# Layer norm scalars moved to GpSimd without a reciprocal, the mean taken from the product's accumulator, the softmax sums' addition in the accumulating form, and new priorities

## The chip, the cores and the metric

One core of one Trainium2 chip runs the kernel. Its engines are PE (TensorE, matrix products), DVE (VectorE), ACT (ScalarE), POOL (GpSimd) and SP (SyncE, which here only issues DMAs). Each engine works through its own instructions in order, and waits on semaphores where another engine or a DMA must come first. The metric is the device time of one execution in microseconds (us), the median of several.

## The reference

Block-causal attention over 8 batches, 8 heads, 576 positions of 64 values, in blocks of 64, then one dense layer pair on 4608 tokens of 512 values, with a SoLU activation and a layer norm between:

```python
scores = scale * np.matmul(q, k.transpose(0, 1, 3, 2))
scores = np.where(block_i >= block_j, scores, -1000000000.0)
scores = scores - np.max(scores, axis=-1, keepdims=True)
attn = np.exp(scores)
attn = attn / (np.sum(attn, axis=-1, keepdims=True) + 1e-09)
x = np.matmul(attn, v)              # then (tokens, 512)
h = x @ w_in                        # (4608, 1024)
e = np.exp(h - np.max(h, axis=-1, keepdims=True))
solu = h * e / (np.sum(e, axis=-1, keepdims=True) + 1e-09)
mu = np.mean(solu, axis=-1, keepdims=True)
var = np.mean((solu - mu) ** 2, axis=-1, keepdims=True)
out = ((solu - mu) / np.sqrt(var + 1e-06) * g_ln) @ w_out
```

## The kernel before

**Attention.** Two heads make a pair; there are 32 pairs, and the first four are done in two parts. For a pair, q and k come by DMA into `qz` and `kz`, which hold two pairs at a time and exist once, so that they are loaded anew every second pair. DVE transposes them there (L535), and ACT, POOL and DVE split each into a high and a low part (`qh`, `ql`, `kh`, `kl`, L536 to L542; the diagonal copies `qdh` and `qdl` for the last 64 rows, L546). PE multiplies three products per score tile (L576; the last 64 rows of both heads in L570) into PSUM. DVE takes each row's maximum (`nm`, L605), ACT the exponential with its sum (`pb`, `z`, L617). DVE adds 1e-9 and inverts the sums (L627, L628), and the rows are scaled on POOL, DVE or ACT (L635 to L637). Except for the first eight pairs, DVE transposes `pb` in blocks (L643) and SP moves it to `pt` (L651). PE multiplies `pt` by `vr` (v, loaded by SP, L475 and L479): the attention product, L663, 52 instructions a pair. Its result is copied from PSUM to `xt` (L417 on ACT or L418 on DVE).

**The two dense layers ("MoE" in the names).** 36 tiles of 128 tokens. `xh` and `xl` are the high and low part of x (L726, L730). PE multiplies by `w_in` in two halves of 12 matmuls (L751, bank `ps` of two). DVE takes the maximum (L757), ACT the exponential with its sum in `m1` (L758), DVE the product h * e with its sum (L759, `m2`). L760 turns the sum into minus the mean, and L766 or L767 adds it to the tile `ub`. ACT squares with a sum (L769, `m4`). L772 to L774 work out 1/z and 1/(z * z * 1024), L777 the variance, and POOL the power -0.5 and the product with 1/z (L780, L781); that number scales the output (L825 or L826). For tiles 4 to 34 DVE transposes `ub` to `zb` (L787) and SP moves it to `ct` (L791); then come its high and low part, `ch` and `cl` (L799 to L803), and the product with `w_out` in two halves of 12 matmuls (L821). The other tiles are transposed on PE (L809).

**PSUM.** Two double banks (1024 columns; `ps_61`, `ps_62` in the order) take the tiles of L751 and L570; four single banks (`ps_63` to `ps_66`) take scores, attention products, output products and PE transposes, each as it comes free.

**The order** is not written by hand. A list scheduler in the kernel (`Schedule.run`) goes through a time of its own. Whenever an engine is free it takes, among the operations whose inputs are there, the one with the smallest key: a pair's or tile's number plus a constant of `PARAMS` for that kind of operation. Operations with alternatives may go to another engine (the constants that begin with `a_`, added to the key). `port=True` marks DVE operations that the scheduler does not let run beside POOL. All engines then execute the recorded order, whatever the real times are. The weights are split into parts in the same way at the start (`prep`, L355 to L385).

## Time and profile before

| what | value |
|---|---|
| median of the runs | 718.22 us (717.61 to 718.95, 3 runs) |
| the profiled execution | 716.22 us, its span 714.3 us |
| mean granted PE clock | 0.970 |
| instructions | 14282 |

A line of a group reads: line, engine, operation, written and read tensor, shape, count | busy us in all, mean ns of one | idle time of the engine just before them, and what ended it. A line of the timeline reads: start us, length us, engine, line, operation, and in brackets the idle time before it and its releaser. SPq is SP issuing a DMA. Line numbers are those of the kernel before.

### The profile page before, as it was taken

The page shows a single profiled execution, that of the slowest core. Times are in us where ns is not written, and L with a number is a line of the kernel's source. Part 1 is how long each engine was busy: PE and PEld are TensorE (multiplying, and loading weights), DVE is VectorE, ACT ScalarE, POOL GpSimd, SP SyncE. Part 2 cuts the span into 40 slices and gives each one's busy share as a digit, 9 for nine tenths or more (in the row PEclk, how much of TensorE's full clock was granted, in tenths as well). Part 3 has the DMA queues.
Part 4 walks back from the last instruction along what each step waited for, and adds up shares of the span by engine and source line. Part 5 has one row for each costly group of instructions (what it writes and reads, how often), then busy time and mean ns, then how long its engine had stood idle before and what let it go on. Part 6 is the DMA issues. An engine that isn't in the chain of part 4 may idle for free.

```text
span 714.3 us, 14282 instructions
## 1 busy us (share of the span) xinstructions
PE 673.9 (94%) x4747; PEld 530.8 (74%) x4747; DVE 593.2 (83%) x1353; ACT 453.7 (64%) x1136; POOL 353.3 (49%) x497
## 2 busy tenths in 40 slices
PE   5879979999989999999999998999999899999997
PEld 5657767877767877777777776777777677888886
DVE  2888999998989999898989997979898898555652
ACT  3888898876686657566666665666656566333332
POOL 2257567552555475555656565454646553133210
PEclk8698979999999999999999999999999999999999
...
GB/s 181 191 94 131 115 127 110 143 187 160 157 186 170 178 191 195 174 178 176 192 179 191 163 194 173 179 157 180 179 170 183 167 175 160 122 71 86 63 74 45
DMA packets 223434, 109.74 MB, mean 154 GB/s; under 512 B 186496, under 2 KB 202368, under 8 KB 223360
## 3 DMA queue, kind: packets, MB, share of 16 engines
...
## 4 chain that ended last, share of the span: by engine, by line
PE 29%; DVE 23%; DMA 6%; ACT 5%; issue 5%; SPq 4%; POOL 1%; DVEq 0%; POOLq 0%; ACTq 0%
PE ps L821 12%; PE ps L751 11%; DVE pb L643 6%; DMA qz<-in_q_dram 5%; DVE nm L605 5%; SPq L464 4%; PE ps L663 3%; DVE ms L757 2%; DVE ub L759 2%; PE ps L576 2%; ACT pb L637 2%; ACT pb L617 2%; DVE zb L787 1%; DVE qz L535 1%; ACT ub L758 1%
## 5 line engine op out<-in xcount | busy, mean ns | idle before, releaser
L617 ACT ACTIVATE pb<-ps,nm 128x256 f32<-128x256 f32 (+4 forms) x288 | 157.2, 554 | 103.0 <-DVE nm L605 69.7
L605 DVE TENSOR_REDUCE nm<-ps 128x1 f32<-128x256 f32 (+4 forms) x288 | 132.6, 507 | 0.2
L643 DVE STREAM_TRANSPOSE pb<-pb 128x1536 f32<-128x1536 f32 (+1 forms) x56 | 101.5, 1827 | 2.3 <-ACT pb L637 2.1
L663 PEld LDWEIGHTS ps<-pt,vr 128*64 128x64 f32 x1648 | 82.5, 140 | 19.0 <-issue 4.6
L663 PE MATMUL ps<-pt,vr 128*64 128x128 f32 (+1 forms) x1648 | 94.8, 273 | 0.1
L821 PE MATMUL ps<-woh,ch 128*128 128x512 f32 x288 | 81.7, 405 | 9.8 <-ACT pb L617 8.6
L751 PE MATMUL ps<-wih,xh 128*128 128x512 f32 x288 | 82.8, 409 | 4.6 <-DVE ub L759 2.6
L637 ACT ACTIVATE pb<-pb,rz 128x128 f32<-128x128 f32 (+4 forms) x166 | 84.8, 573 | 2.9 <-DVE rz L628 2.8
L803 POOL TENSOR_TENSOR cl<-ct,ch 128x512 fp32r<-128x512 f32 x52 | 66.6, 1289 | 33.9 <-ACT ch L799 30.0
L821 PE MATMUL ps<-wol,ch 128*128 128x512 f32 x288 | 79.5, 398 | 0.0
L821 PE MATMUL ps<-woh,cl 128*128 128x512 f32 x288 | 79.0, 396 | 0.0
L751 PE MATMUL ps<-wil,xh 128*128 128x512 f32 x288 | 78.8, 395 | 0.0
L751 PE MATMUL ps<-wih,xl 128*128 128x512 f32 x288 | 78.6, 394 | 0.0
L821 PEld LDWEIGHTS ps<-woh,ch 128*128 128x128 f32 x288 | 51.4, 189 | 25.2 <-POOL qdh L546 9.0
L751 PEld LDWEIGHTS ps<-wih,xh 128*128 128x128 f32 x288 | 50.9, 188 | 24.7 <-issue 8.4
L576 PE MATMUL ps<-kh,qh 64*128 64x128 f32 (+3 forms) x256 | 57.5, 385 | 9.5 <-ACT pb L617 7.9
L821 PEld LDWEIGHTS ps<-wol,ch 128*128 128x128 f32 x288 | 54.8, 190 | 12.9
L821 PEld LDWEIGHTS ps<-woh,cl 128*128 128x128 f32 x288 | 54.7, 190 | 12.9
L751 PEld LDWEIGHTS ps<-wih,xl 128*128 128x128 f32 x288 | 54.1, 188 | 12.9
L751 PEld LDWEIGHTS ps<-wil,xh 128*128 128x128 f32 x288 | 54.2, 188 | 12.8
L769 ACT ACTIVATE junk<-ub 128x1024 bf16<-128x1024 f32 x31 | 32.8, 1057 | 42.6 <-DVE ub L767 21.0
L758 ACT ACTIVATE ub<-ps,ms 128x1024 f32<-128x1024 f32 x36 | 40.0, 1111 | 29.2 <-DVE ms L757 29.2
...
## 6 DMA issues: line engine op xcount, KB each, us to landing
pt<-pb SPq DMA_DIRECT2D x112, 400.0 KB, 6.1
...
```

Source lines behind the costliest of these rows:

```text
L464: SP.dma_start(dst[32 * g : 32 * g + 32].rearrange("p m (g d) -> p (m g) d", d=32), src[b0, ha + g - g % 2 : ha + g - g % 2 + 2, :, 32 * ( ...
L576: PE.matmul(PS(sps[h])[:, off : off + 128 * (i_ + 1)], w_[half[h], 128 * i_ : 128 * i_ + 128], x_[half[h], 0 : 128 * (i_ + 1)], start=n_ = ...
L605: op("DVE", t_dve(wid[u]), lambda sp=sp, off=off, u=u: DVE.tensor_reduce(out=nm_[u], in_=PS(sp)[:, off : off + wid[u]], axis=AX.X, op=ALU. ...
L617: ACT.activation(dst, src, AF.Exp, bias=nm_[u], accum_out=z_[zg][:, zc : zc + 1])
L637: ("ACT", t_act(nn, 133), lambda b=b, zg=zg, zc=zc: ACT.activation(puv(pb, b, pep), puv(pb, b, pep), AF.Copy, scale=rz_[zg][:, zc : zc + 1 ...
L643: op("DVE", 1.058 * 128 * (s1 - s0) + 86, lambda s0=s0, s1=s1: DVE.transpose(pb[:, :, s0:s1, :], pb[:, :, s0:s1, :]), r=[("P", i, b) for b ...
L663: PE.matmul(dst(PS(av)[half[h]]), w_, pt_[:, a0:a1, sl, :], start=start, stop=stop)
L751: PE.matmul(o_, a_[:, c, :], w_[:, c, s_], start=(si == 0 and c == 0), stop=(si == 2 and c == NKI - 1))
L758: op("ACT", t_act(1024, 186), lambda: ACT.activation(u, PS(hps), AF.Exp, bias=m[:, 0:1], accum_out=m[:, 1:2]), r=[("m0", i)], w=[uk, ("m1" ...
L769: op("ACT", t_act(1024, 135), lambda: ACT.activation(junk, cz, AF.Square, accum_out=m[:, 4:5]), r=[ck], w=[("m4", i)], key=key + K["sq"])
L803: alts=[("POOL", 1225, lambda c_=c_, h_=h_, l_=l_: POOL.tensor_tensor(out=l_, in0=c_, in1=h_.bitcast(F32), op=ALU.subtract), K["a_clo"])])
L821: PE.matmul(o_, a_[:, c, :], w_[:, c, :], start=(hf == 0 and si == 0 and c == 0), stop=(hf == 1 and si == 2 and c == 7))
```

## The change

The variance is worked out without 1/z. With s the sum of h * e, d = h * e - s/1024 and z the sum of e plus 1e-9, the reference's (solu - mu)/sqrt(var + 1e-6) is d / sqrt(mean(d * d) + 1e-6 * z * z). So POOL now makes (z/1000) squared (`zsq`: a tensor_scalar and a product) and then the variance and its power -0.5 (`rstd`: a tensor_scalar and the power), and DVE's five small instructions a tile go. The product h * e carries the factor 1/1024, so that its accumulator is the mean, and the subtraction multiplies by 1024 again. The softmax sums' addition of 1e-9 gets an accumulator output (`zsum`, which nobody reads) and is no longer kept from running beside POOL in the scheduler. All constants of `PARAMS` are new, and there are two more for the new operations; the tables differ in every entry but two.

```diff
--- before.py
+++ after.py
@@ -39,19 +39,19 @@
 PARAMS = {
-    "nd": 2, "ld": 62.912, "lv": -14.91, "q": 350.247, "qe": -0.799, "s": -76.343, "se": 33.052,
+    "nd": 2, "ld": 20.894, "lv": 47.527, "q": -19.234, "qe": -0.357, "s": -89.577, "se": 14.69, "sr": -37.453,
...
-    "a_spA": -161.148, "a_saA": -281.747, "w2": -2.125, "w3": 2.401, "hA": 488.772,
+    "w2": 201.331, "w3": 1560.764, "hA": 16323.164, "zq": 71.846, "rs": -11.826,
 }
@@ -289,6 +289,7 @@
     ob = [sb(f"ob{i}", [DM]) for i in range(2)]
     ms = [sb(f"ms{i}", [8]) for i in range(2)]
     junk = sb("junk", [DFF], mybir.dt.bfloat16)
+    zsum = sb("zsum", [1])
 
     DVE.memset(mhalf, -0.5)
 
@@ -624,11 +625,11 @@
 
                 def recip(zg=zg, z0=z0, z1=z0 + len(bs)):
                     z = z_[zg][:, z0:z1]
-                    DVE.tensor_scalar(out=z, in0=z, scalar1=1e-9, scalar2=None, op0=ALU.add)
+                    DVE.tensor_scalar(out=z, in0=z, scalar1=1e-9, scalar2=0.0, op0=ALU.add, op1=ALU.add, accum_out=zsum)
                     DVE.reciprocal(rz_[zg][:, z0:z1], z)
 
                 zk = [("z", i, u) for u in bs]
-                op("DVE", 300, recip, r=zk, w=[("rz", i, zg)] + zk, key=p + K["sr" + sfx], port=True)
+                op("DVE", 300, recip, r=zk, w=[("rz", i, zg)] + zk, key=p + K["sr" + sfx])
                 for b in bs:
                     nn = P * (b[1] + 1)
                     zc = zcol[b][1]
@@ -756,33 +757,27 @@
         uk = ("ub", i)
         op("DVE", t_dve(1024), lambda: DVE.tensor_reduce(out=m[:, 0:1], in_=PS(hps), axis=AX.X, op=ALU.max, negate=True), w=[("m0", i)], key=key + K["he"], ps=hps)
         op("ACT", t_act(1024, 186), lambda: ACT.activation(u, PS(hps), AF.Exp, bias=m[:, 0:1], accum_out=m[:, 1:2]), r=[("m0", i)], w=[uk, ("m1", i)], key=key + K["he"], ps=hps)
-        op("DVE", t_dve(1024), lambda: DVE.scalar_tensor_tensor(out=u, in0=PS(hps), scalar=1.0, in1=u, op0=ALU.mult, op1=ALU.mult, accum_out=m[:, 2:3]), r=[uk], w=[uk, ("m2", i)], key=key + K["he"], ps=hps)
-        op("DVE", 65, lambda: DVE.tensor_scalar(out=m[:, 3:4], in0=m[:, 2:3], scalar1=-1.0 / DFF, scalar2=None, op0=ALU.mult), r=[("m2", i)], w=[("m3", i)], key=key + K["he"])
+        op("DVE", t_dve(1024), lambda: DVE.scalar_tensor_tensor(out=u, in0=PS(hps), scalar=1.0 / DFF, in1=u, op0=ALU.mult, op1=ALU.mult, accum_out=m[:, 2:3]), r=[uk], w=[uk, ("m2", i)], key=key + K["he"], ps=hps)
         dst, src, ck, cw = u, u, uk, [uk]
         if not t in BT:
             dst, src = (x.rearrange("p (c a b) -> p c a b", a=a_, b=P // a_) for x, a_ in ((zb, 32), (u, 4)))
             src = src.rearrange("p c r j -> p c j r")
             cw, ck = ["zb"], "zb"
-        op("POOL", 1097, lambda: POOL.tensor_scalar(out=dst, in0=src, scalar1=m[:, 3:4], scalar2=1.0, op0=ALU.add, op1=ALU.mult), r=[uk, ("m3", i)] + (wkeys if t == 0 else []), w=cw, key=key + K["c"],
-           alts=[("DVE", 713 if dst is u else 1250, lambda: DVE.tensor_scalar(out=dst, in0=src, scalar1=m[:, 3:4], scalar2=1.0, op0=ALU.add, op1=ALU.mult), K["a_c"])], port=True)
+        op("POOL", 1097, lambda: POOL.tensor_scalar(out=dst, in0=src, scalar1=float(DFF), scalar2=m[:, 2:3], op0=ALU.mult, op1=ALU.subtract), r=[uk, ("m2", i)] + (wkeys if t == 0 else []), w=cw, key=key + K["c"],
+           alts=[("DVE", 713 if dst is u else 1250, lambda: DVE.tensor_scalar(out=dst, in0=src, scalar1=float(DFF), scalar2=m[:, 2:3], op0=ALU.mult, op1=ALU.subtract), K["a_c"])], port=True)
         cz = u if t in BT else zb
         op("ACT", t_act(1024, 135), lambda: ACT.activation(junk, cz, AF.Square, accum_out=m[:, 4:5]), r=[ck], w=[("m4", i)], key=key + K["sq"])
 
-        def rz():
-            DVE.tensor_scalar(out=m[:, 1:2], in0=m[:, 1:2], scalar1=1e-9, scalar2=None, op0=ALU.add)
-            DVE.reciprocal(m[:, 5:6], m[:, 1:2])
-            DVE.tensor_scalar(out=m[:, 6:7], in0=m[:, 5:6], scalar1=m[:, 5:6], scalar2=1.0 / DFF, op0=ALU.mult, op1=ALU.mult)
-
-        def var():
-            DVE.tensor_scalar(out=m[:, 7:8], in0=m[:, 4:5], scalar1=m[:, 6:7], scalar2=1e-6, op0=ALU.mult, op1=ALU.add)
+        def zsq():
+            POOL.tensor_scalar(out=m[:, 5:6], in0=m[:, 1:2], scalar1=1e-9, scalar2=1e-3, op0=ALU.add, op1=ALU.mult)
+            POOL.tensor_tensor(out=m[:, 6:7], in0=m[:, 5:6], in1=m[:, 5:6], op=ALU.mult)
 
         def rstd():
-            POOL.tensor_tensor(out=m[:, 4:5], in0=m[:, 7:8], in1=mhalf, op=ALU.pow)
-            POOL.tensor_tensor(out=m[:, 3:4], in0=m[:, 4:5], in1=m[:, 5:6], op=ALU.mult)
-
-        op("DVE", 527, rz, r=[("m1", i)], w=[("m5", i), ("m1", i)], key=key + K["sq"])
-        op("DVE", 129, var, r=[("m4", i), ("m5", i)], w=[("m7", i)], key=key + K["sq"])
-        op("POOL", 772, rstd, r=[("m7", i), ("m5", i)], w=[("m4", i), ("m3", i)], key=key + K["sq"])
+            POOL.tensor_scalar(out=m[:, 7:8], in0=m[:, 4:5], scalar1=1.0 / DFF, scalar2=m[:, 6:7], op0=ALU.mult, op1=ALU.add)
+            POOL.tensor_tensor(out=m[:, 3:4], in0=m[:, 7:8], in1=mhalf, op=ALU.pow)
+
+        op("POOL", 380, zsq, r=[("m1", i)], w=[("m6", i)], key=key + K["zq"])
+        op("POOL", 1000, rstd, r=[("m4", i), ("m6", i)], w=[("m3", i)], key=key + K["rs"])
         if t in BT:
             op("DVE", t_dve(DFF), lambda: DVE.transpose(zb.rearrange("p (r c i) -> p r c i", r=4, i=32), u.rearrange("p (c r i) -> p r c i", r=4, i=32)), r=[uk] + (wkeys if t == BT[0] else []), w=["zb"], key=key + K["ct"])
 
```

Lines after the change stand one lower than before from L293 on, and five lower from L787 on (L787 is L782, L821 is L816).

With the new constants the order of all engines is another. Three places:

SP's queue in the middle of the kernel, one period of two pairs, from the block move of the odd pair's `pb` (`pt_91`; `pt_90` is the even pair's; `vr_80` and `vr_81` likewise; `ob` is an output tile). Before:

```order
L651 DMA pt_91<-pb_89 128x1x800 x4
L475 DMA vr_80<-in_v_dram 128x4x64 x2
L479 DMA vr_80<-in_v_dram 64x2x64
L827 DMA out_dram<-ob_131 128x512
L791 DMA ct<-zb 128x1x256 x4
L464 DMA kz<-in_k_dram 32x36x32 x4
L464 DMA qz<-in_q_dram 32x36x32 x4
L475 DMA vr_81<-in_v_dram 128x4x64 x2
L479 DMA vr_81<-in_v_dram 64x2x64
```

After, from the load of `vr_80`, which must wait for the even pair's attention product that still reads it:

```order
L476 DMA vr_80<-in_v_dram 128x4x64 x2
L480 DMA vr_80<-in_v_dram 64x2x64
L652 DMA pt_91<-pb_89 128x1x800 x4
L786 DMA ct<-zb 128x1x256 x4
L822 DMA out_dram<-ob_131 128x512
L465 DMA kz<-in_k_dram 32x36x32 x4
L465 DMA qz<-in_q_dram 32x36x32 x4
L652 DMA pt_90<-pb_88 128x1x800 x4
L476 DMA vr_81<-in_v_dram 128x4x64 x2
L480 DMA vr_81<-in_v_dram 64x2x64
```

The load of v for the even pair moved ahead of the move of `pb`, and the output ahead of k and q moved behind `ct`.

DVE at the transposes of k and q in such a period (`nm` are the row maxima of the odd pair). Before:

```order
L535 STREAM_TRANSPOSE kz<-kz 128x576 x2
L760 TENSOR_SCALAR ms_132<-ms_132 128x1
L535 STREAM_TRANSPOSE qz<-qz 128x576 x2
L787 STREAM_TRANSPOSE zb<-ub 128x1024
L601 MEMSET ps_66 64x64
L601 MEMSET ps_63 64x64
L601 MEMSET ps_65 64x64
L605 TENSOR_REDUCE nm_01_102<-ps_66 128x1
```

After, from the last maximum of the first score group:

```order
L606 TENSOR_REDUCE nm_10_105<-ps_66 128x1
L594 MEMSET ps_61 128x64
L782 STREAM_TRANSPOSE zb<-ub 128x1024
L536 STREAM_TRANSPOSE qz<-qz 128x576 x2
L606 TENSOR_REDUCE nm_24_109<-ps_61 128x1
L602 MEMSET ps_64 64x64
L602 MEMSET ps_63 64x64
L606 TENSOR_REDUCE nm_01_102<-ps_64 128x1
L606 TENSOR_REDUCE nm_11_106<-ps_63 128x1
```

The MoE transpose `zb` moved ahead of the q transpose, the k transpose lies further up, and the maximum of the last 64 rows (`nm_24`) stands behind the q transpose.

PE in this stretch: before, the pairs alternate between two orders (after the attention product of the even pair L576 with 6 instructions, half an L751, 6 of L576, half an L751, half an L821, then the odd pair's L663, after which come 6 of L570, 12 of L576, half an L821, half an L751, 12 of L576, half an L751, half an L821, 12 of L576, 6 of L570 and half an L821). After, every pair has the same order: L663, 6 of L570, 12 of L576, half an L821, half an L751, 12 of L576, half an L751, half an L821.

ACT at the start, around the first exponentials (L367 casts weights, L371 scales them; `kh`, `qh` are the first pairs' keys and queries). Before:

```order
L417 ACTIVATE qh_82<-ps_65 128x256
L367 ACTIVATE ob_130<-ub 128x512
L617 ACTIVATE pb_88,z_0_110<-ps_63,nm_01_93 128x256
L617 ACTIVATE pb_88,z_0_110<-ps_63,nm_00_92 128x128
L617 ACTIVATE pb_88,z_0_110<-ps_64,nm_11_97 128x256
L617 ACTIVATE pb_88,z_0_110<-ps_64,nm_10_96 128x128
L371 ACTIVATE zb<-zb 128x512
L637 ACTIVATE pb_88<-pb_88,rz_0_114 128x256 x2
```

After:

```order
L418 ACTIVATE qh_82<-ps_65 128x256
L368 ACTIVATE ob_130<-ub 128x512
L368 ACTIVATE ob_131<-ub 128x512
L372 ACTIVATE zb<-zb 128x512
L618 ACTIVATE pb_88,z_0_110<-ps_63,nm_01_93 128x256
L618 ACTIVATE pb_88,z_0_110<-ps_63,nm_00_92 128x128
L618 ACTIVATE pb_88,z_0_110<-ps_64,nm_11_97 128x256
L618 ACTIVATE pb_88,z_0_110<-ps_64,nm_10_96 128x128
```

A second cast and the scaling moved ahead of the first four exponentials.

11 lines of the change are left out of this document (6 added, 5 removed), and 11 rows, old and new, of the table PARAMS.

## The prediction

> **What bounds the kernel.** I read the busy times, then a table of stretches, TensorE's own waits, the spacing of the attention products, and last the queues around one wait. The first fence is the page's busy line, then the stretches (columns: length, busy us of PE, weight load, DVE, ACT, POOL with instruction counts, granted clock, DMA share, GB/s), then PE's longest wait between 200 and 600 us (total, times, longest).
>
> ```profile
> PE 673.9 (94%) x4747; PEld 530.8 (74%) x4747; DVE 593.2 (83%) x1353; ACT 453.7 (64%) x1136; POOL 353.3 (49%) x497
> ...
> 0.00:150.00 150.00, 127.45 (x1061) 101.71 (x1061) 125.27 (x311) 117.01 (x298) 79.14 (x120) 0.87 0.68 138
> 150.00:200.00 50.00, 46.07 (x358) 35.70 (x357) 44.88 (x98) 34.90 (x95) 20.90 (x33) 1.00 0.86 167
> 200.00:600.00 400.00, 390.11 (x2782) 304.30 (x2782) 362.03 (x834) 262.16 (x678) 228.32 (x313) 1.00 0.90 180
> 600.00:714.30 114.30, 110.29 (x556) 89.12 (x550) 61.05 (x112) 39.65 (x68) 24.91 (x33) 0.99 0.28 77
> ...
> PE ps L821 <- ACT pb L617: 8.6, 7, 2.8
> ```
>
> TensorE is the bound: its matmuls are fixed, so only its idle time can go: 22.6 us before 150 us, 3.9 to 200, 9.9 to 600, 4.0 in the tail, and what the clock of 0.87 costs at the start. From 200 to 600, 8.6 of the 9.9 us are one wait, an output product (L821) waiting for the softmax exponential (L617) to leave its PSUM bank.
>
> How fast could the middle be? The attention products (L663) mark the pairs. The first and the fourth row are eight double pairs apart, the two between are the even and the odd pair of one of them; the last four rows, from the chain of work, are one pair in which PE never waits.
>
> ```profile
> 270.02 2.98 PE L663 MATMUL ps<-pt,vr 128*64 128x128 f32 x52
> ...
> 529.68 2.98 PE L663 MATMUL ps<-pt,vr 128*64 128x128 f32 x52
> ...
> 542.79 2.98 PE L663 MATMUL ps<-pt,vr 128*64 128x128 f32 x52
> ...
> 568.61 2.98 PE L663 MATMUL ps<-pt,vr 128*64 128x128 f32 x52
> ...
> 581.78 2.90 PE ps L663 x52
> ...
> 592.73 1.25 PE ps L576 x12
> ...
> 596.96 2.80 PE ps L821 x12
> 599.75 2.90 PE ps L663 x52
> ```
>
> Measured: (568.61 - 270.02)/8 = 37.32 us for two pairs. PE alone needs 599.75 - 581.78 = 17.97 a pair, 35.94 for two. The difference is 1.38 us, 11.1 us over the eight; I call it the stall.
>
> Where it comes from is seen at its worst place. SP's queue, then DVE, ACT and PE at the same moment (start, length; in brackets the idle time before it and who ended it):
>
> ```profile
> 530.78 7.11 SPq L651 DMA_DIRECT2D pt<-pb  x4
> 537.99 2.80 SPq L475 DMA_DIRECT2D vr<-in_v_dram  x2
> ...
> 542.21 2.51 SPq L791 DMA_DIRECT2D ct<-zb  x4
> 544.84 4.06 SPq L464 DMA_DIRECT2D kz<-in_k_dram  x4
> 549.30 3.33 SPq L464 DMA_DIRECT2D qz<-in_q_dram  x4
> ...
> 556.98 1.44 DVE L535 STREAM_TRANSPOSE qz<-qz 128x576 f32<-128x576 f32 x2 [3.39 <-DMA qz<-in_q_dram]
> 558.34 1.20 DVE L787 STREAM_TRANSPOSE zb<-ub 128x1024 f32<-128x1024 f32 x1
> ...
> 560.15 0.47 ACT L617 ACTIVATE pb<-ps,nm 128x256 f32<-128x256 f32 x1 [3.42 <-DVE nm L605]
> ...
> 560.86 1.18 PE L821 MATMUL ps<-woh,ch 128*128 128x512 f32 x4 [2.82 <-ACT pb L617]
> ```
>
> DVE is not short of time here. It stands 3.39 us at the q transpose until the q load lands, and behind it in order stand the MoE transpose (1.20) and the row maxima that the exponential needs; so PE stands 2.82. The load is late because SP issues in order, almost without a pause, from 530.78 to 552.63: pt, v, an output, ct, k, q. The arrival of q against PE's need of a bank decides the middle, and DVE's total load only helps around it.
>
> **The change, part by part.** Rows are groups: busy us, mean ns, idle before. Those with 128x6 and 128x3 keep shapes apart.
>
> ```profile
> L760 DVE TENSOR_SCALAR ms<-ms 128x1 f32<-128x1 f32 x36 | 5.1, 141 | 3.2 <-ACT ob L825 3.2
> L772 DVE TENSOR_SCALAR ms<-ms 128x1 f32<-128x1 f32 x36 | 5.3, 147 | 10.2 <-ACT ub L758 10.2
> L773 DVE RECIPROCAL ms<-ms 128x1 f32<-128x1 f32 x36 | 5.9, 164 | 1.7
> L774 DVE TENSOR_SCALAR ms<-ms 128x1 f32<-128x1 f32 x36 | 7.7, 214 | 1.3
> L777 DVE TENSOR_SCALAR ms<-ms 128x1 f32<-128x1 f32 x36 | 6.3, 174 | 2.2 <-ACT junk L769 2.2
> L780 POOL TENSOR_TENSOR ms<-ms,mhalf 128x1 f32<-128x1 f32 x36 | 22.5, 625 | 69.7 <-DVE ms L777 64.3 <-DVE ms L772 4.6
> L781 POOL TENSOR_TENSOR ms<-ms 128x1 f32<-128x1 f32 x36 | 7.0, 196 | 2.8
> L864 POOL MEMSET const-float32-0.0<- 128x1 f32 x1 | 0.1, 98 | 0.2 <-issue 0.2
> L635 POOL TENSOR_SCALAR pb<-pb,rz 128x128 f32<-128x128 f32 x8 | 3.8, 480 | 5.2 <-ACT pb L617 2.9 <-DVE rz L628 1.4 <-ACT zb L371 0.8
> L627 DVE TENSOR_SCALAR z<-z 128x6 f32<-128x6 f32 x28 | 10.0, 358 | 3.0 <-ACT pb L617 3.0
> L627 DVE TENSOR_SCALAR z<-z 128x3 f32<-128x3 f32 x32 | 5.4, 168 | 1.5 <-ACT pb L617 1.4
> L759 DVE DVE_READ_ACCUMULATOR ub<-ps,ub 128x1 f32 x36 | 3.0, 83 | 0.0
> L418 DVE TENSOR_SCALAR xt<-ps 128x192 f32<-128x192 f32 (+3 forms) x43 | 16.3, 399 | 1.6 <-PE ps L663 1.3
> L800 POOL TENSOR_SCALAR ch<-ct 128x512 fp32r<-128x512 f32 x28 | 17.3, 619 | 54.9 <-DMA ct<-zb 40.2 <-PE ps L821 6.6 <-PE ps L570 6.0
> ```
>
> *Scalars.* DVE loses five instructions a tile, 141 + 147 + 164 + 214 + 174 = 840 ns, 30.2 us over 36 tiles. The 1/1024 inside L759 is an immediate and costs nothing. POOL loses 625 + 196 and gains a power (625), a product (196) and two tensor_scalars of one element, which no row shows: 98 (memset of that size) to 480 (128 wide), so 7 to 35 us in all; I take 200 each, as the product of that size, 14 us. POOL has 171 us idle from 200 to 600, which covers them. It also no longer waits for DVE's variance (64.3 us of idle at L780); it waits for ACT's square sum instead, and behind that wait stand the next pair's keys. These have from the pair's last score to the end of the next attention product, 592.73 + 1.25 to 599.75 + 2.90, 8.7 us.
>
> *Softmax sums.* In the accumulating form a sum costs 168 to 358 plus 83 ns to read the accumulator. At 251 ns all 68 together cost what they cost now: 28 x (251 - 358) + 40 x (251 - 168) = +0.3 us. Were the form to keep the 358 ns at width 6, it is 28 x 83 + 3.3 = +5.6 us of DVE, a tenth of what the change frees. The Trainium skill (SBUF — State Buffer, "Who interferes with whom") says tensor_scalar may take the port pair shared with GpSimd, but not in the form that writes its accumulator. The gap between 358 and 168 fits such waiting, though no run yet shows the other form; by the page it is +0.3, by the row +5.6.
>
> *Regrouping by the priorities.* By the order, all 43 PSUM copies of L418 to xt leave DVE (16.3 us) for ACT, as do 9 output scalings; all 11 mean subtractions that DVE did and 24 copies of L800's kind (24 x 619 = 15 us) go to POOL. Counted with the row means of before, DVE falls by about 65 us (estimate), POOL rises by about 50, ACT by about 8. From 200 to 600 ACT is busy 262 us and POOL 228, so the larger loads are hidden; that cover would be gone only if one stood for a whole pair.
>
> *The middle.* Two pairs now have PE's order of the quoted 17.97 us pair twice, so its PE time is 35.94. Set the even pair's L663 at 0. Before, PE wanted the bank at 560.86 - 2.82 - 529.68 = 28.4 (the odd pair's L663 starts 542.79 - 529.68 = 13.1 behind the even one). After, the odd pair's L663 stands at 17.97, and the product in question is the one that starts 596.96 - 581.78 behind it: PE wants the bank at 33.2, 4.8 us later. SP's order is now v, pt, ct, out, k, q. v must wait for L663 to end (2.9); v and the output took 542.21 - 537.99 = 4.2, and with pt 7.1, ct 2.5, k 4.1 and q 3.3 the last q issue ends at 24.1, against 552.63 - 529.68 = 22.9 before. It landed 556.98 - 552.63 = 4.35 later: 28.5. The bank came free 560.86 - 556.98 = 3.9 after that: 32.4, inside 33.2. So even the worst stall goes, with 0.8 us to spare. I take 9 of the 11.1 us as gained (ends: none, if SP is slower still, and all). From 150 to 270 there are 5 us more of idle time; half, 2.5 (0 to 5).
>
> *The start and the end.* Up to 150 us DVE (125.3) and ACT (117.0) are both nearly full. The new order reads the raw q and k chunks ahead of v, about 10 us earlier in SP's queue, but lets ACT do two weight casts and a scaling ahead of the first exponentials, which wait anyway:
>
> ```profile
> 14.85 0.66 ACT L367 ACTIVATE ob<-ub 128x512 int32<-128x512 uint32 x1 [3.70 <-DMA ub<-in_moe_w_in_dram]
> ...
> 16.36 0.58 PE L576 MATMUL ps<-kh,qh 64*128 64x256 f32 x2 [5.81 <-ACT pb L617]
> ...
> 704.87 0.96 PE L821 MATMUL ps<-woh,ch 128*128 128x512 f32 x3 [0.44 <-ACT ch L812]
> ```
>
> The second cast costs 0.66, the scaling taken alike: some 1.3 us later at the first exponential, earlier at the full pairs. I take 0, with ends of -6 and +6, a quarter of the 22.6 us. In the last tile the transposes move between two halves of the product ahead; the 0.44 us wait goes.
>
> **Sum.** The profiled execution took 716.22 us, span 714.3 plus 1.9; it is 2.0 below the median of the runs, 718.22. 716.2 - 9 - 2.5 - 0 - 0.4 = 704.3; with the 2.0, 706.5 for the median.
>
> **Rivals.** *The attention product waits for pt (slower).* v now stands ahead of pt in SP's queue and itself waits for L663. pt's last issue ends at 2.9 + 4.2 + 7.1 = 14.2 at the latest, 3.8 us before its product at 17.97; before it was 530.78 + 7.11 = 537.89 against 542.79, 4.9, and PE did not wait. Should pt land 3 us late, two pairs take 38.9; over eight that is 8 x (38.9 - 37.32) = +13 in place of -9: 716.2 + 13 - 2.9 + 2.0, about 728. It decides from 1.4 us on. For it: the margin shrinks by 1.1 us; against it: PE nowhere waits for pt now, and the two-pair time on which SP's work is spread stays 36 us.
>
> *Nothing gained.* DVE's freed time is not what PE waits for; if q lands 2 us later than worked out, the stall is the same and the change measures 717 to 719. Within this: longer waits at the port, if POOL's 50 us lengthen the remaining two-port DVE work. The Trainium skill (Perfetto Trace Analysis, "Optimizing Scalar/DVE Operations") says that moving work between DVE and GpSimd might not help because of that port. The width-6 row shows such a price, 0.19 us; on some 200 instructions it is 38 us of DVE, of the 65, so DVE would still be lighter.
>
> *A worse start.* 5 us lost before 150 us, with PE's clock low for longer: 711 to 716.
>
> **Chances.** Forecast 0.60 (its own range 698 to 712), worse start 0.14, nothing gained 0.11, slower 0.15. The range of 698 to 720 leaves out the slower case and a little above its ends. A measurement here can tell about 0.2%, 1.4 us, from no change: the first two cases give faster 0.74; nothing gained gives same 0.10 and the last hundredth to slower, 0.16.
>
> **What would show it.** Right: L663 spaced by 36.0 us for two pairs; PE idle from 200 to 600 under 3 us; the wait for the q load without PE behind it; DVE near 530, POOL near 400, ACT near 460 us busy; L777's line at 625 ns with a much shorter wait. Wrong: L663 waiting for a DMA, a POOL wait reaching the scores, or PE idle above 25 us before 150.

## The result: 738.22 us, 2.8% slower

The changed kernel takes 738.22 us (median of 4, 736.31 to 740.92), the kernel before 718.59 beside it (717.61 to 719.19): a ratio of 1.0277, 95% interval 1.0239 to 1.0315. The forecast was 706.5 with a range of 698 to 720, so it is wrong, in sign too. The profiled execution took 736.31 us, with a span of 734.5, 20.2 more than before. In the changed kernel the lines up to the product h * e carry a number one higher than before (L663 is now L664, L759 now L760), L766 and L769 keep theirs, and those behind the scalars are five lower (L787 is now L782, L821 now L816). L772 and L773 are now GpSimd's scaled z and its square, L776 the variance, L777 the power. All 36 subtractions of the mean are L766.

The busy line, and the same four stretches that the prediction showed for before:

```profile
PE 680.0 (93%) x4747; PEld 533.2 (73%) x4747; DVE 534.5 (73%) x1188; ACT 455.7 (62%) x1155; POOL 491.3 (67%) x603
...
0.00:150.00 150.00, 119.05 (x1032) 94.44 (x1032) 111.90 (x292) 114.48 (x297) 85.17 (x122) 0.90 0.68 137
150.00:200.00 50.00, 46.32 (x327) 35.30 (x329) 43.96 (x104) 34.09 (x92) 21.64 (x32) 1.00 0.73 159
200.00:600.00 400.00, 390.74 (x2787) 305.13 (x2783) 334.67 (x735) 259.91 (x676) 298.35 (x364) 0.99 0.85 175
600.00:734.50 134.50, 123.86 (x608) 98.31 (x606) 43.94 (x59) 47.25 (x92) 86.11 (x86) 0.99 0.30 83
```

DVE fell by 59 us, nearly as forecast (530 expected, 534.5 came), ACT is at 456 (460 expected). POOL is at 491 where "near 400" was expected: some 91 us too many. So one of POOL's prices is wrong, and the groups say which (busy us, mean ns, idle before):

```profile
L766 POOL TENSOR_SCALAR ub<-ub,ms 128x1024 f32<-128x1024 f32 x31 | 115.5, 3726 | 16.9 <-DVE ub L760 15.4
...
L766 POOL TENSOR_SCALAR zb<-ub,ms 128x1024 f32<-128x1024 f32 x5 | 24.4, 4890 | 6.5 <-DVE qz L536 6.1
...
L777 POOL TENSOR_TENSOR ms<-ms,mhalf 128x1 f32<-128x1 f32 x36 | 20.5, 570 | 10.0 <-ACT ob L820 4.7 <-DMA pt<-pb 2.8
...
L776 POOL TENSOR_SCALAR ms<-ms 128x1 f32<-128x1 f32 x36 | 10.4, 288 | 6.1 <-ACT junk L769 6.1
```

In the profile of before L766 took:

```profile
L766 POOL TENSOR_SCALAR ub<-ub,ms 128x1024 f32<-128x1024 f32 x21 | 23.6, 1122 | 42.6 <-DVE ms L772 33.1 <-DVE ms L760 9.4
...
L766 POOL TENSOR_SCALAR zb<-ub,ms 128x1024 f32<-128x1024 f32 x4 | 8.6, 2156 | 1.5 <-DVE nm L605 1.1 <-PE ps L809 0.3
```

Same line, same shapes, same engine: 3726 ns in place of 1122, and 4890 in place of 2156 where the copy also regroups. What differs is the pair of operations: before (add a pointer, multiply by 1.0), now (multiply by 1024, subtract a pointer). 31 x 2.604 + 5 x 2.734 = 94.4 us more than at the old price, which is the surplus within the roundness of "near 400". The other new pieces came near their terms: the power at 570 ns for 625, with 10.0 us of idle time ahead of it in place of 69.7, the variance at 288 for 200.

Who waits for it (all of the span: total us, times, longest):

```profile
ACT junk L769 <- POOL ub L766: 97.8, 30, 5.2
DVE zb L782 <- POOL ub L766: 77.3, 27, 8.2
...
ACT junk L769 <- POOL zb L766: 18.9, 5, 6.1
```

And one such moment, of POOL, ACT, DVE and PE (start, length, in brackets the idle time before and its releaser):

```profile
560.15 3.71 POOL L766 TENSOR_SCALAR ub<-ub,ms 128x1024 f32<-128x1024 f32 x1 [1.06 <-DVE ub L760]
...
563.90 1.06 ACT L769 ACTIVATE junk<-ub 128x1024 bf16<-128x1024 f32 x1 [4.76 <-POOL ub L766]
564.86 0.19 ACT L769 ACTIVATION_READ_ACCUMULATOR junk<-ub 128x1 f32 x1
564.95 0.56 ACT L618 ACTIVATE pb<-ps,nm 128x384 f32<-128x384 f32 x1
...
561.93 1.39 DVE L606 TENSOR_REDUCE nm<-ps 128x1 f32<-128x384 f32 x4
...
566.92 1.07 PE L577 MATMUL ps<-kh,qh 64*128 64x512 f32 x2
```

ACT's sum of squares (L769) is next in ACT's queue and needs the centred tile, so ACT stands 4.76 us. The score exponentials stand behind it, although their row maxima (L606) are ready by 563.3. They run from 564.95 to 566.9, and the next score products can only start when a PSUM bank is read out: the two of 566.92 take 1.07 us together. In the version of experiment 2, without the slow form, the same two take:

```profile
556.84 0.40 PE L577 MATMUL ps<-kh,qh 64*128 64x512 f32 x2
```

PE's recorded waits for these exponentials from 200 to 600 us, first the changed kernel, then the version of experiment 2 (total us, times, longest):

```profile
PE ps L577 <- ACT pb L618: 3.3, 13, 0.6
```

```profile
PE ps L577 <- ACT pb L618: 0.8, 3, 0.4
```

A "double" below is the time of two pairs, as in the prediction: an eighth of the time between two attention products that are eight double pairs apart (the twentieth and the fourth from the end). In the changed kernel:

```profile
277.11 2.98 PE L664 MATMUL ps<-pt,vr 128*64 128x128 f32 x52
...
574.16 2.98 PE L664 MATMUL ps<-pt,vr 128*64 128x128 f32 x52
```

(574.16 - 277.11)/8 = 37.13 us, against 37.32 before and 36.0 forecast. By these lines alone one would say that the middle stayed as it was and the start (277.11 against 270.02) and the end lost. That reading is misleading, as experiment 2 shows: without the slow instruction the middle does gain.

### The profile page after: what moved, and what is told of

Same layout as the page of the kernel before. It is cut to its first block, busy times and chain, and to the rows that moved or that the text cites. A ratio compares the mean times of both kernels' runs of the same rounds, so it can differ in the third digit from the quotient of the medians.

```text
span 734.5 us, 14226 instructions
## 1 busy us (share of the span) xinstructions
PE 680.0 (93%) x4747; PEld 533.2 (73%) x4747; DVE 534.5 (73%) x1188; ACT 455.7 (62%) x1155; POOL 491.3 (67%) x603
## 4 chain that ended last, share of the span: by engine, by line
PE 22%; POOL 21%; ACT 15%; DVE 15%; DMA 11%; issue 8%; SPq 7%; ACTq 0%; POOLq 0%; DVEq 0%
POOL ub L766 10%; PE ps L752 8%; ACT pb L618 7%; PE ps L816 6%; DVE pb L644 4%; DMA ct<-zb 4%; PE ps L664 4%; PE ps L577 3%; POOL cl L798 3%; ACT pb L638 3%; SPq L786 3%; SPq L465 3%; POOL zb L766 3%; DMA qz<-in_q_dram 2%; DVE nm L606 2%
## 5 line engine op out<-in xcount | busy, mean ns | idle before, releaser
L618 ACT ACTIVATE pb<-ps,nm 128x256 f32<-128x256 f32 (+4 forms) x288 | 157.2, 556 | 55.0 <-DVE nm L606 45.2
L606 DVE TENSOR_REDUCE nm<-ps 128x1 f32<-128x256 f32 (+4 forms) x288 | 132.6, 507 | 0.4
L766 POOL TENSOR_SCALAR ub<-ub,ms 128x1024 f32<-128x1024 f32 x31 | 115.5, 3726 | 16.9 <-DVE ub L760 15.4
L644 DVE STREAM_TRANSPOSE pb<-pb 128x1536 f32<-128x1536 f32 (+1 forms) x56 | 103.0, 1839 | 19.1 <-ACT pb L638 11.9
L638 ACT ACTIVATE pb<-pb,rz 128x384 f32<-128x384 f32 (+4 forms) x158 | 88.1, 617 | 27.8 <-DVE rz L629 27.7
L782 DVE STREAM_TRANSPOSE zb<-ub 128x1024 f32<-128x1024 f32 x31 | 38.6, 1246 | 79.4 <-POOL ub L766 77.3
L664 PEld LDWEIGHTS ps<-pt,vr 128*64 128x64 f32 x1648 | 80.2, 137 | 20.2 <-issue 8.5
L769 ACT ACTIVATE junk<-ub 128x1024 bf16<-128x1024 f32 x31 | 32.8, 1058 | 97.8 <-POOL ub L766 97.8
L664 PE MATMUL ps<-pt,vr 128*64 128x128 f32 (+1 forms) x1648 | 92.6, 269 | 0.9 <-ACT pb L618 0.9
L816 PE MATMUL ps<-woh,ch 128*128 128x512 f32 x288 | 84.2, 415 | 5.7 <-ACT ch L794 3.5
L798 POOL TENSOR_TENSOR cl<-ct,ch 128x512 fp32r<-128x512 f32 x59 | 76.0, 1289 | 20.0 <-ACT ch L794 16.1
L816 PE MATMUL ps<-wol,ch 128*128 128x512 f32 x288 | 80.2, 401 | 0.0
L816 PE MATMUL ps<-woh,cl 128*128 128x512 f32 x288 | 79.2, 397 | 0.0
L577 PE MATMUL ps<-kh,qh 64*128 64x128 f32 (+3 forms) x256 | 65.0, 382 | 13.3 <-ACT pb L618 7.5
L816 PEld LDWEIGHTS ps<-woh,ch 128*128 128x128 f32 x288 | 52.8, 193 | 19.4 <-ACT ch L794 4.0
L816 PEld LDWEIGHTS ps<-wol,ch 128*128 128x128 f32 x288 | 55.6, 193 | 13.2
L816 PEld LDWEIGHTS ps<-woh,cl 128*128 128x128 f32 x288 | 54.7, 190 | 13.0
```

The source lines that it names most:

```text
L577: PE.matmul(PS(sps[h])[:, off : off + 128 * (i_ + 1)], w_[half[h], 128 * i_ : 128 * i_ + 128], x_[half[h], 0 : 128 * (i_ + 1)], start=n_ = ...
L606: op("DVE", t_dve(wid[u]), lambda sp=sp, off=off, u=u: DVE.tensor_reduce(out=nm_[u], in_=PS(sp)[:, off : off + wid[u]], axis=AX.X, op=ALU. ...
L618: ACT.activation(dst, src, AF.Exp, bias=nm_[u], accum_out=z_[zg][:, zc : zc + 1])
L638: ("ACT", t_act(nn, 133), lambda b=b, zg=zg, zc=zc: ACT.activation(puv(pb, b, pep), puv(pb, b, pep), AF.Copy, scale=rz_[zg][:, zc : zc + 1 ...
L644: op("DVE", 1.058 * 128 * (s1 - s0) + 86, lambda s0=s0, s1=s1: DVE.transpose(pb[:, :, s0:s1, :], pb[:, :, s0:s1, :]), r=[("P", i, b) for b ...
L664: PE.matmul(dst(PS(av)[half[h]]), w_, pt_[:, a0:a1, sl, :], start=start, stop=stop)
```

## Experiments

"Form" below is the theory that GpSimd's price of L766 makes the loss. Its rivals are the new order itself, and the scalars on GpSimd. Unless said otherwise an experiment keeps the changed kernel's order of instructions on every engine. "Span" is that of the profiled execution; ratios are to the kernel before, run beside it, with 95% intervals.

**1. The mean part undone.**

```diff
-scalar_tensor_tensor(out=u, scalar=1.0 / DFF, ..., accum_out=m[:, 2:3])
+scalar_tensor_tensor(out=u, scalar=1.0, ..., accum_out=m[:, 2:3])
+DVE.tensor_scalar(out=m[:, 2:3], in0=m[:, 2:3], scalar1=-1.0 / DFF, op0=ALU.mult)
-POOL.tensor_scalar(scalar1=float(DFF), scalar2=m[:, 2:3], op0=ALU.mult, op1=ALU.subtract)
+POOL.tensor_scalar(scalar1=m[:, 2:3], scalar2=1.0, op0=ALU.add, op1=ALU.mult)
```

> The new order and all the rest of the change, with the mean part alone undone: the product is accumulated without 1/1024, VectorE forms minus the mean in one more instruction of one element a tile (36 of them), and the subtraction on GpSimd is again (add a pointer, multiply by 1.0). Theory 'form' (the form with the multiplication by an immediate first and the pointer second is what costs GpSimd 2.6 us a tile, and those 94 us are the loss): the 31 subtractions fall from 3.73 us to about 1.12 and the 5 regrouping ones from 4.89 to about 2.16, GpSimd's busy time from 491 us to about 400, and the time to 703 to 712 us, as the prediction had it. Rival 'order' (the new priorities themselves lose the time): 733 us or more, whatever GpSimd's busy time does. Rival 'scalars' (the small GpSimd operations hold up the chain): 728 us or more. Anything between 713 and 728 would be shared among them.

Measured: 699.68 us, ratio 0.9724 (0.9661 to 0.9786), span 698.1. L766 is at 1142 and 2180 ns, POOL at 395.9 us. The form theory holds. The time came out 3 us below its span of expectations; the order and the scalars are not the loss.

**2. The mean kept in the accumulator, with its sign turned.**

```diff
-scalar=1.0 / DFF          (the product)
+scalar=-1.0 / DFF
-scalar1=float(DFF),  scalar2=m[:, 2:3], op0=ALU.mult, op1=ALU.subtract
+scalar1=-float(DFF), scalar2=m[:, 2:3], op0=ALU.mult, op1=ALU.add
```

> The product is accumulated with -1/1024, so that the accumulator holds minus the mean, and the subtraction becomes (multiply by -1024, add the pointer), with no further instruction. If the cost lies in the operation 'subtract', L766 falls to about 1.1 us (2.2 regrouping) and the time to 702 to 710 us. If it lies in the place of the pointer (an immediate first, a pointer second), L766 stays at 3.7 (4.9) and the time at 735 to 741 us. The one-element row of the changed kernel in this form (L776: 288 ns against 191 to 193 ns for its neighbours) speaks for the second, which I take at 0.65.

Measured: 700.38 us, ratio 0.9739 (0.9672 to 0.9807), span 695.1. This is not the outcome that I took at 0.65: what counts is the operation, not the pointer's place.

```profile
L766 POOL TENSOR_SCALAR ub<-ub,ms 128x1024 f32<-128x1024 f32 x31 | 35.4, 1142 | 12.5 <-DVE ub L760 10.2
...
L766 POOL TENSOR_SCALAR zb<-ub,ms 128x1024 f32<-128x1024 f32 x5 | 11.5, 2293 | 6.8 <-DVE nm L606 6.4
```

With the same order on every engine and the same count of instructions, a changed sign and one word (`add` for `subtract`) take 39.4 us off the span of the profiled execution, 37.8 off the median. It also beats the kernel before by 2.6%; I call it the cheap version. Its stretches and attention products:

```profile
0.00:150.00 150.00, 123.15 (x1072) 98.35 (x1073) 119.92 (x310) 118.69 (x309) 78.15 (x125) 0.92 0.72 143
150.00:200.00 50.00, 47.87 (x370) 37.03 (x369) 44.19 (x106) 36.84 (x98) 23.27 (x38) 1.00 0.81 176
200.00:600.00 400.00, 398.50 (x2912) 315.37 (x2911) 342.54 (x744) 269.22 (x697) 247.12 (x377) 1.00 0.88 183
```

```profile
260.76 2.98 PE L664 MATMUL ps<-pt,vr 128*64 128x128 f32 x52
...
545.69 2.98 PE L664 MATMUL ps<-pt,vr 128*64 128x128 f32 x52
```

Doubles of (545.69 - 260.76)/8 = 35.62 us, PE idle 1.5 us from 200 to 600. Since the orders are the same, the 39.4 us can be split by place: 277.11 - 260.76 = 16.4 up to that product, 13.2 to the last attention product (624.89 against 595.36), 9.9 from there to the end.

**3. The form alone, in the kernel before.** Product with 1/1024 and L766 (and VectorE's L767) as (multiply by 1024, subtract the pointer); L760 stays, though nothing needs its result, so that the order is as before.

```diff
-scalar=1.0, in1=u, ..., accum_out=m[:, 2:3]
+scalar=1.0 / DFF, in1=u, ..., accum_out=m[:, 2:3]
-scalar1=m[:, 3:4], scalar2=1.0, op0=ALU.add, op1=ALU.mult
+scalar1=float(DFF), scalar2=m[:, 2:3], op0=ALU.mult, op1=ALU.subtract
```

> The kernel before, in its own order, with only the new form: the product accumulated with 1/1024 and the subtraction as (multiply by 1024, subtract the pointer); the small instruction that formed minus the mean stays as dead work, so that nothing else moves. Theory 'form': GpSimd's 25 subtractions rise to 3.7 us (4.9 for the regrouping four), GpSimd's busy time from 353 to about 418 us, and the time by 8 to 25 us, to 726 to 743 us (0.9 us for each of the 25, by the 32 us that the 36 cost by this theory, less where VectorE's eleven cover). VectorE's eleven stay at 0.78 us, or rise too, which no run has shown yet. Rival 'order': the time stays within 717 to 721 us.

Measured: 752.12 us, ratio 1.0446 (1.0366 to 1.0526), span 751.3, POOL 418.5 us as expected. The direction is the form theory's, the size is above its upper end of 743: 33 us for 25 slow instructions, 1.3 each, where the 36 of the changed kernel cost 1.1 each. The price on VectorE stayed:

```profile
L766 POOL TENSOR_SCALAR ub<-ub,ms 128x1024 f32<-128x1024 f32 x21 | 78.0, 3714 | 33.5 <-DVE ub L759 32.4
...
L766 POOL TENSOR_SCALAR zb<-ub,ms 128x1024 f32<-128x1024 f32 x4 | 18.8, 4698 | 0.6 <-PE ps L809 0.3
...
L767 DVE TENSOR_SCALAR ub<-ub,ms 128x1024 f32<-128x1024 f32 x10 | 7.8, 780 | 0.0
```

**4 and 5. Tables of prices.** L766 by the tile's number in several forms (first table), each on its own line; in the second also the two-tensor residues. Both compute other numbers than the reference and ran once each; only their prices are read.

> A table of prices: the changed kernel with the subtraction in six forms in turn (by the tile's number modulo 6), each on a line of its own: (multiply 1024, subtract pointer), (multiply 1024, add pointer), (add pointer, multiply 1024), (subtract pointer, multiply 1024), the first one on VectorE, and (multiply 1024, subtract an immediate). Its output is not the reference's, since four of the forms compute another number. If the pointer's place decides: 3.7, 3.7, 1.1, 1.1 us on GpSimd, and 1.1 with two immediates. If 'subtract' decides: 3.7, 1.1, 1.1, 3.7, and 3.7 with two immediates. If multiplying by 1024 instead of 1.0 decides: 3.7 in all five on GpSimd. On VectorE 0.78 us, as for the other form, or more. The time of the whole lies between 705 and 738 us and decides nothing.

> More prices on GpSimd, in the changed kernel's order, with output that is not the reference's: the subtraction L766 by the tile's number modulo 3 as two halves of 512 in the slow form, as 'subtract the pointer' alone with no second operation, and as 'add the pointer' alone; and the two-tensor residues of the layer norm (128x512, 1.29 us) as subtract, add and multiply by turns. If the slow form costs per element: 1.9 us a half (3.7 for both); if it is a fixed 2.6 us: 3.2 us a half. 'Subtract' alone 3.6 us against 1.1 for 'add' alone if the operation decides by itself. The two-tensor instructions cost the same in all three (1.25 to 1.35 us) if the slowness belongs to the form with a scalar; if 'subtract' is slow everywhere, add and multiply take 0.6 to 0.7 us.

First table: L770 (multiply, subtract pointer), L772 (multiply, add pointer), L774 (add pointer, multiply), L776 (subtract pointer, multiply), L779 (multiply, subtract an immediate), L778 as L770 on VectorE:

```profile
L770 POOL TENSOR_SCALAR ub<-ub,ms 128x1024 f32<-128x1024 f32 x5 | 19.0, 3800 | 2.6 <-DVE ub L760 2.4
L776 POOL TENSOR_SCALAR ub<-ub,ms 128x1024 f32<-128x1024 f32 x5 | 18.6, 3715 | 1.6 <-DVE ub L760 1.2
L779 POOL TENSOR_SCALAR ub<-ub 128x1024 f32<-128x1024 f32 x5 | 18.2, 3643 | 3.6 <-DVE ub L760 3.4
...
L772 POOL TENSOR_SCALAR ub<-ub,ms 128x1024 f32<-128x1024 f32 x5 | 5.6, 1125 | 1.5 <-DVE ub L760 1.2
...
L774 POOL TENSOR_SCALAR ub<-ub,ms 128x1024 f32<-128x1024 f32 x5 | 5.6, 1123 | 2.5 <-DVE ps L594 1.1 <-DVE ub L760 1.1
...
L778 DVE TENSOR_SCALAR ub<-ub,ms 128x1024 f32<-128x1024 f32 x6 | 4.4, 728 | 0.0
```

Second table: L773 is "subtract the pointer" alone, L775 "add the pointer" alone, L770 and L771 halves of 512 in the slow form, L811 to L813 two-tensor subtract, add and multiply:

```profile
L773 POOL TENSOR_SCALAR ub<-ub,ms 128x1024 f32<-128x1024 f32 x11 | 31.4, 2854 | 6.0 <-DVE ub L760 4.9 <-DVE ps L594 1.1
...
L775 POOL TENSOR_SCALAR ub<-ub,ms 128x1024 f32<-128x1024 f32 x10 | 28.6, 2864 | 3.8 <-DVE ub L760 3.8
L812 POOL TENSOR_TENSOR cl<-ct,ch 128x512 fp32r<-128x512 f32 x22 | 28.4, 1292 | 7.3 <-ACT ch L806 5.5 <-PE ps L831 0.5
...
L813 POOL TENSOR_TENSOR cl<-ct,ch 128x512 fp32r<-128x512 f32 x19 | 24.4, 1289 | 5.5 <-ACT ch L806 4.3
...
L811 POOL TENSOR_TENSOR cl<-ct,ch 128x512 fp32r<-128x512 f32 x18 | 23.2, 1290 | 7.1 <-ACT ch L806 5.3 <-PE ps L831 0.7
...
L770 POOL TENSOR_SCALAR ub<-ub,ms 128x512 f32<-128x512 f32 x10 | 20.5, 2053 | 4.3 <-DVE ub L760 3.6
...
L771 POOL TENSOR_SCALAR ub<-ub,ms 128x512 f32<-128x512 f32 x10 | 20.0, 1999 | 0.9
```

My "subtract decides" is right for pairs and too narrow. A pair of add and multiply, in either order and with 1.0 or 1024, is fast at 1.12 us. A pair with subtract takes 3.6 to 3.8, with a pointer in either place, and with an immediate second (an immediate subtracted first was not tried). A single operation, which I had expected at 1.1 for add, takes 2.86, add as much as subtract. So the multiplication by 1.0 in the kernel before, which changes no number, goes with the fast price: the same addition without it is the slow one. Why GpSimd's price depends on the operations in this way no run shows. The slow pair costs by the element: (3726 - 2026)/512 = 3.3 ns an element between the halves and the whole, with the mean of the two halves. Two-tensor instructions take 1.29 us with each of the three operations. On VectorE the pair with subtract costs 728 ns.

**6. The same form on VectorE** at the same 36 places.

```diff
-op("POOL", 1097, lambda: POOL.tensor_scalar(out=dst, ...
+op("POOL", 1097, lambda: DVE.tensor_scalar(out=dst, ...
```

> The changed kernel with the same subtraction, same form (multiply by 1024, subtract the pointer), at the same 36 places, issued on VectorE instead of GpSimd (728 ns there by the table of prices, some 1.25 us for the five that regroup): VectorE's busy time from 534 to about 563 us, GpSimd's from 491 to about 351. If the loss is GpSimd's price of this form and nothing else: 699 to 708 us, since VectorE at 556 us still gave 702. If the new order itself can't bear it: 715 us or more.

Measured: 700.79 us, ratio 0.9765 (0.9723 to 0.9807), span 696.7, DVE 563.5 and POOL 351.8 us, as expected. The 31 take 902 ns each there and the five that regroup 1304, more than the 728 of the table. So the form as such is harmless; its price on GpSimd is the loss.

**7. Slow only in the five tiles that regroup**, beside the cheap version (`BT` are the tiles that do not).

```diff
-scalar=-1.0 / DFF
+scalar=(-1.0 if t in BT else 1.0) / DFF
-scalar1=-float(DFF), ..., op1=ALU.add
+scalar1=-float(DFF) if t in BT else float(DFF), ..., op1=ALU.add if t in BT else ALU.subtract
```

> The version with the cheap subtraction, in which the five regrouping ones alone (the first four tiles and the last) have the slow form, 4.89 us instead of 2.29. If these five make the loss of the start and a part of the end, as the changed kernel's first 270 us, 16 us behind the cheap version's, suggest: 707 to 715 us, with doubles of 35.6 us unchanged. If the loss there came from the later tiles' 3.7 us as well: 701 to 706 us.

Measured: 710.92 us, ratio 0.9902 (0.9871 to 0.9934), span 712.8, L766 at 4907 ns for these five and 1138 for the others. The attention product that stands at 260.76 in the cheap version and at 277.11 in the changed kernel stands at 274.86: with four slow instructions ahead of it, 10.5 us more of GpSimd (4 x (4907 - 2293) ns), it is 14.1 of the 16.4 us late. That is more than the five cost by the medians, 710.92 - 700.38 = 10.5 us: the profiled execution of this run is the slowest of its five (714.62), that of the cheap version the fastest of its four. So the five carry most of the start's loss, and how much exactly is open. There `zb` exists once and PE transposes from it:

```profile
ACT junk L769 <- POOL zb L766: 16.3, 5, 6.1
...
PEld ps L804 <- POOL zb L766: 7.5, 4, 2.6
...
PE ps L804 <- POOL zb L766: 6.1, 4, 2.1
```

The doubles are 35.89 us, 0.27 above the cheap version's.

**8. ScalarE freed of the wait**, the subtraction still slow, in the changed kernel.

```diff
-ACT.activation(junk, cz, AF.Square, accum_out=m[:, 4:5])
+ACT.activation(junk, wih[:, 0, :].bitcast(F32), AF.Square, accum_out=m[:, 4:5])
```

> How the slow subtraction reaches PE: the changed kernel in its own order with the subtraction still slow on GpSimd, but ScalarE's sum of squares (L769) reads a block of the weights instead of the centred product, so that ScalarE no longer stands for GpSimd there (97.8 + 18.9 us of waiting in the changed kernel); the variance, and so the scale of the rows, is another number. If the loss goes by ScalarE, whose score exponentials stand behind L769 in its queue: 712 to 726 us, of 738. If it goes by VectorE's transposition of the centred product (77.3 us of waiting, score maxima behind it) or by GpSimd's own queue (loads' residues and probabilities behind the subtraction): 730 us or more. I take ScalarE at 0.55.

Measured: 726.18 us, ratio 1.0099 (1.0062 to 1.0136), span 726.0. It lands on the upper edge of what ScalarE's way was to give (726): 12 of the 38 us. By place, in a profiled execution 1.6 us above the median: doubles of 36.32 us (37.13 and 35.62 with and without the slow form), the start 275.19, the end no shorter than the changed kernel's. So ScalarE carries about half of the middle's loss, and next to nothing of the start's and the end's. The rest waits elsewhere:

```profile
ACT pb L618 <- DVE nm L606: 98.4, 46, 4.1
DVE zb L782 <- POOL ub L766: 78.8, 27, 8.7
```

VectorE's transposition still stands for L766, with score maxima behind it, and the exponentials now wait for the maxima 98.4 us, where they did 45.2 in the changed kernel. How the rest divides between VectorE's wait and GpSimd's own queue was not tried.

**9 and 10. Operations and order apart.** The new operations (cheap form) with the old table of priorities, and the old operations with the new table; the planner lays out each anew.

```diff
 # operations without order: the cheap version with the table of before
+"zq": 77.238, "rs": 77.238,
 # order without operations: the kernel before with the changed kernel's table
```

> The new operations without the new priorities: the table of numbers of the kernel before (the two new entries take the value of the old entry 'sq', 77.238), the small scalars on GpSimd, the sums in the accumulating form, the mean from the accumulator in the cheap form (multiply by -1024, add the pointer: 1.14 us). The planner lays its order anew and puts 21 subtractions on GpSimd and 15 on VectorE. If the operations bring the gain of 18 us that the cheap form showed: 700 to 705 us. If the new priorities bring it: 714 to 720 us. I take a part each as likeliest, 705 to 714, since VectorE loses about 40 us of work either way, and before waited for it.

> The new priorities without the new operations: the kernel before with the new table of numbers alone. The planner puts all 36 subtractions on GpSimd in their old form (1.12 us), so VectorE loses about 9 us to GpSimd, and keeps its reciprocals and scalars (some 540 to 580 us busy). If the priorities bring the gain: 700 to 707 us. If the operations bring it: 714 to 722 us, or more, since these numbers were not made for these operations.

Measured: 758.96 us, ratio 1.061 (1.0553 to 1.0667), and 737.14 us, ratio 1.0301 (1.0253 to 1.035). The first missed all its cases; the second's time lies in its "or more", but not by the reason given there, for the operations alone don't bring the gain either. Each half alone costs 21 us or more, and together (experiment 2) they gain 18. The loss is not in the middle: the new order alone has doubles of 35.45 us, the shortest of all runs, and the new operations with the old table of (597.37 - 308.21)/8 = 36.1, both below the 37.32 of before. It is in the start and the end: the twentieth product from the end stands at 282.2 with the order alone and at 308.2 with the operations alone (270.02 before), and behind the last attention product come 120.0 and 111.6 us (100.4 before). So a gain of the middle does not need both, and the numbers of a table fit the operations they were made for, at the first tiles and the last above all.

**11. The scalars back on VectorE** in the cheap version (four instructions a tile), at the places of the GpSimd pieces.

```diff
 def zsq():
-    POOL.tensor_scalar(out=m[:, 5:6], in0=m[:, 1:2], scalar1=1e-9, scalar2=1e-3, op0=ALU.add, op1=ALU.mult)
-    POOL.tensor_tensor(out=m[:, 6:7], in0=m[:, 5:6], in1=m[:, 5:6], op=ALU.mult)
+    (the three of the old rz, on DVE)
 def rstd():
-    POOL.tensor_scalar(out=m[:, 7:8], in0=m[:, 4:5], scalar1=1.0 / DFF, scalar2=m[:, 6:7], op0=ALU.mult, op1=ALU.add)
-    POOL.tensor_tensor(out=m[:, 3:4], in0=m[:, 7:8], in1=mhalf, op=ALU.pow)
+    (the old var on DVE, the two of the old rstd on POOL)
```

> The version with the cheap subtraction (700.4 us), its order kept, with the layer norm's scalars alone put back: the addition, the reciprocal, the product and the variance's multiply-add on VectorE, the power and one product on GpSimd, at the places in the order where the GpSimd pieces stood. VectorE's busy time rises by 144 instructions of 147 to 214 ns, about 25 us, to 558; GpSimd's falls by about 10. If the scalars matter by VectorE's load (the prediction's step b): the doubles of two pairs lengthen from 35.6 us to 36.2 or more and the time to 706 us or more. If PE alone sets the time by then: 699 to 703 us. I take the first at 0.6, since the reciprocal now waits on VectorE ahead of the next pair's score maxima.

Measured: 702.04 us, ratio 0.9811 (0.9768 to 0.9854), span 701.5; DVE 556.0, POOL 379.2. The time is within the second case, not the one taken at 0.6, and the intervals of this and of experiment 2 overlap, so the worth of moving the scalars is not settled by it: 0 to some 5 us. Doubles are 35.91.

**12. The softmax sums' addition without accumulator** in the cheap version.

```diff
-DVE.tensor_scalar(out=z, in0=z, scalar1=1e-9, scalar2=0.0, op0=ALU.add, op1=ALU.add, accum_out=zsum)
+DVE.tensor_scalar(out=z, in0=z, scalar1=1e-9, scalar2=None, op0=ALU.add)
```

> The version with the cheap subtraction (700.4 us, span 695.1 in its profile), order kept, with the softmax sums' addition alone put back to the form without accumulator: 358 and 168 ns instead of 150 and 118 plus 82 for the accumulator's read. Over 64 pairs that is some 4 us more on VectorE, which is not the bound: 699 to 703 us either way. A rise above 704 would show that the wait inside the old form (its 358 ns for six elements) sat on the path of the probabilities.

Measured: 704.24 us, ratio 0.9804 (0.9781 to 0.9827), span 702.6: just above the 704 that was to show a cost, with an interval that overlaps experiment 2's, so a gain of some 4 us for the accumulating form is likely and not settled. VectorE's price is clear, first the cheap version, then this one:

```profile
L628 DVE DVE_READ_ACCUMULATOR z<-z 128x1 f32 x68 | 5.6, 83 | 0.0
...
L628 DVE TENSOR_SCALAR_CACHE_REDUCE z<-z 128x6 f32<-128x6 f32 x28 | 4.3, 153 | 3.4 <-ACT pb L618 3.0
...
L628 DVE TENSOR_SCALAR_CACHE_REDUCE z<-z 128x3 f32<-128x3 f32 x32 | 3.8, 118 | 0.8 <-ACT pb L618 0.8
```

```profile
L628 DVE TENSOR_SCALAR z<-z 128x3 f32<-128x3 f32 x32 | 18.4, 575 | 0.8 <-ACT pb L618 0.8
...
L628 DVE TENSOR_SCALAR z<-z 128x6 f32<-128x6 f32 x28 | 10.4, 370 | 3.0 <-ACT pb L618 2.5
```

The old form takes 575 ns for three elements in this order and 168 in the order of before, so most of it is a wait, not work; VectorE's busy time is 553.0 against 533.4 us.

## Why the prediction was wrong, by its steps

*The step that failed* is the mean subtraction. The prediction said of the mean part "The 1/1024 inside L759 is an immediate and costs nothing", which is so (L760 now takes 1197 ns). What failed is the other half of the same edit: the multiplication by 1024 and the subtraction in L766 got no price of their own. Under "Regrouping by the priorities" it only let "all 11 mean subtractions that DVE did" go to POOL, "Counted with the row means of before", that is at 1122 and 2156 ns for another pair of operations. The right term was +94 us of GpSimd for the 36, and +39.4 us of the span, 37.8 by the medians (experiment 2). For an operation that the trace of before does not show, the prediction set bounds elsewhere (the small scalars); here it took a changed instruction for a moved one.

*The cover.* That "the larger loads are hidden; that cover would be gone only if one stood for a whole pair" was false. L766 stands 3.7 us, a fifth of a pair, and the engine that waits for it has the next scores' exponentials queued behind. POOL had 102 us idle from 200 to 600 even so; what cost time was the length of one instruction and what is queued behind its readers. The way by ScalarE is shown for about half of the middle's loss (experiment 8) and the way by the five regrouping tiles for most of the start's (experiment 7); the rest of the way is open.

*The middle*, without the slow form, went as worked out. Doubles of 36.0 were forecast and 35.62 came; the gain over eight is 13.7 us, where 9 was taken and 11.1 was the upper end, since the pair of before that gave the floor of 17.97 was 0.16 us longer than the 17.81 now seen. The wait named as the cause went: DVE waits for the q load 17.2 us from 200 to 600 before, and 0.6 in the cheap version (total us, times, longest):

```profile
DVE qz L535 <- DMA qz<-in_q_dram: 17.2, 9, 3.4
```

```profile
DVE qz L536 <- DMA qz<-in_q_dram: 0.6, 1, 0.6
```

It went in experiments 9 and 10 too (1.6 and 2.5 us), so the gain is not the new order's alone. In the changed kernel L766 ate it.

*Scalars.* DVE's relief was right (22.6 us of busy time came back with the four of experiment 11, 5.5 us with L760's in experiment 1; 30.2 forecast for the five) and so was GpSimd's +14 us: 192 + 195 + 286 + 554 = 1227 ns a tile in the cheap version against 821, times 36 is 14.6. Their worth in time is small and open (experiment 11).

*Softmax sums.* The size was off, in the favourable direction: 118 to 153 plus 83 ns, not 168 to 358 plus 83. The Trainium skill (SBUF — State Buffer, "Who interferes with whom") says that the form which writes its accumulator cannot take the port pair shared with GpSimd. The traces agree: at three and six elements the instruction with accumulator keeps to 117 to 157 ns in all runs, and without it the groups' means run from 168 to 575.

*Start and end.* Forecast as 0 and -0.4. In the cheap version all that lies outside the eight doubles is 5.5 us shorter than before, 2.9 forecast. That this is near is luck, since two misses stand in it: up to the twentieth product from the end 9.3 us are gained (270.02 against 260.76; 2.5 were forecast), and the three pairs behind the doubles take 4.3 us more (49.67 against 45.33). That PE's clock is granted at 0.95 from 40 to 110 us against 0.85 before goes with the shorter start, though the changed kernel, with the longer one, has 0.95 there too. "PE idle above 25 us before 150" was a badly chosen sign: the changed kernel has 31.0, but the cheap version also has 26.9.

*Rivals.* None is what happened. No wait of PE for pt shows from 200 to 600 in the changed kernel or the cheap version, and the 700 us of experiment 2 exclude "nothing gained" for the change at the right price. The changed kernel has the worse start, 7.1 us, but mainly by the regrouping L766 (experiment 7), not by the casts. Of the signs named for "wrong", two came: PE's idle time before 150, and a POOL wait that reaches the scores, by way of ACT.

In sum, 704.3 was forecast for the profiled execution, a span of 702.4; 695.1 came in experiment 2, where L766 has the price that the prediction counted with, and 39.4 on top of it in the changed kernel. By the medians it is 706.5, 700.38 and 738.22.
